# The first two MLP groups run half by half, each half in accumulators of its own; and a new order of x's loads and VectorE's reads

## The chip, the cores and the metric

The kernel runs on one core of a Trainium2 chip. The metric is device time in microseconds (us) of one execution; lower is better. Besides the runs that give the time there is one profiled execution, from which the profile and the trace come. Engines are called by the profile's names: PE (TensorE, matrix products), ACT (ScalarE), DVE (VectorE), POOL (GpSimd) and SP (SyncE, which here only issues DMAs).

## The reference, cut to what matters

A token is a row of 512 numbers; there are 2048. The function normalises x, takes a two-dimensional Fourier transform (real part) by products with the given matrices, puts the same normalised x through an MLP, and joins the two:

```python
xn = _layernorm(x)                                   # x: 2048 x 512
a, b = xn @ dft_hid_re.T, xn @ dft_hid_im.T          # hidden DFT
s = dft_seq_re @ a - dft_seq_im @ b                  # sequence DFT, real part
y = _layernorm(xn)
h = _gelu(y @ w1 + b1)                               # 1792 units
g = _silu(h @ w2 + b2)
return x + s * g
```

## The kernel before, in words

Every fp32 factor is split in two parts, a rounded high one (made by ACT) and the rest as a low one (made by DVE, which needs the high one first); a product is then three matmuls, high by high, high by low and low by high (`split_into`, L63 to L65). The larger products are done in seven block products instead of eight (Strassen's scheme in Winograd's form), so sums and differences of the blocks are made on DVE first.

Tokens come in four blocks of 512, in the order `TB = (0, 2, 1, 3)`. The stages that the change touches, in order:

1. **Hidden DFT of blocks 0 and 2 (of `TB`), L369 to L561.** `x_load` loads x by tiles of 128 tokens, `xt_load` loads transposed blocks. The first four tiles are transposed on PE; the mean and variance of the others come from DVE (`stats`, L110, L111) or, for tokens 12 to 15, from ACT (`act_stats`, L310, L311). A row of means (`m_pack`, `m_turn`: a transpose on PE, a copy on ACT, a write to DRAM from ACT's queue and a load back to all partitions on SP's queue, named `rsm`, `rpm`, `rtm`, `rdm`, `rowm`) is subtracted from the transposed block (L269). `second_factors` (L140) turns the variances into factors, which PE transposes (`rpR`, L166).
2. **Hidden DFT of the other two blocks, L577 to L595**, by seven products of rows (`q_product`, L514), each over four column blocks c. `q_after` reads an accumulator to SBUF (ACT for products 1, 5, 6, 4, DVE L502 for 2, 3, 7). The steps that DVE and ACT do between the products are listed in the calls: `post` (reads), `y_scale`, `y_sum`, `y_split` (the MLP's right factors: "11", "12", "21", "22", and the sums "t1" to "t4", each for the two halves tau = 0 and 1 of the token blocks), `a_split` (weights of the DFT), `w1_sums`, `w1_split`, `w1_load` (the MLP's weights of one group).
3. **MLP, first layer, L599 to L980**: seven groups j of units. A group takes seven products p in the order 1, 5, 6, 2, 3, 7, and 4 later, behind the next group's first two; each is for both halves tau (`TAUS`), twelve matmuls. Products 1, 6, 7, 4 add up in accumulator `hy`, 5 and 3 in `hz`, 2 in `hx`. Behind each `h_product` (L626) stands `h_after`: ACT copies out after products 1, 5 and 6 (L639), DVE adds after 2, 3 and 7 (L669, L675, L679), and ACT applies gelu (L631). Group 0 alone runs by halves, `ONE` (tau 1) and then `ZERO` (tau 0), in the same accumulators, and `y_late` puts the right factors of tau 0 that are not yet made between its products. POOL's queue stores the results, SP's loads and stores the rest.
4. The MLP's second layer, the sequence DFT and the gate follow (L960 to L1141).

The program is run in the order in which it is written (`manual_schedule`): each engine and queue works off its own instructions in that order, and waits where an operand, a buffer or an accumulator is not ready. `yp` has four tiles of two banks for the MLP's accumulators; `wr` holds one group's raw weights; `op` holds 39 tiles that are handed out again when their last user is done.

```python
h_seq = [(0, p, s) for s in (ONE, ZERO) for p in (1, 5, 6, 2, 3, 7)]
for j in range(1, NJ):
    h_seq += [(j, 1, TAUS), (j, 5, TAUS), (j - 1, 4, TAUS), (j, 6, TAUS), (j, 2, TAUS), (j, 3, TAUS), (j, 7, TAUS)]
```

Of the kernel before, what the change touches and what calls it, by code (L numbers as in the profile page):

```python
# [22 lines left out]
def fnet_mixer_kernel(ctx: ExitStack, tc: tile.TileContext, x, xT, ct, wt, w1, w2, b1, b2, out):  # L23
    nc = tc.nc
# [354 lines left out]
    for q in range(NC):  # L379
        x_load(NC + q)  # L380
    for q in (12, 13, 8, 9):
        x_load(q)
    xt_load(1)
    for q in (14, 15, 10, 11):
        x_load(q)
# [12 lines left out]
    m_turn()  # L398
    for q in range(12, 15):
        act_stats(q)  # L400
# [125 lines left out]
    for i in range(3, HB):  # L526
        if i == 3:
            xt_prepare(1)
            act_stats(15)
            for q in (10, 11):  # L530
                stats(mv1, xs[q], q)
            neg_means(2)
            neg_means(0)
        if i == 4:
            second_factors()
        if i == 5:
            a_sums()
# [27 lines left out]

    def w1_make(j):
        w1_sums(j)
        w1_split(j)
        w1_load(j + 1)
# [46 lines left out]

    def h_product(j, p, taus=TAUS):
        key = {1: "y", 2: "x", 5: "z", 3: "z", 6: "y", 7: "y", 4: "y"}[p]
        if (j, key) not in hx:
            hx[j, key] = acc_two(f"h{key}{j}")  # L620
        acc, (wh, wl) = hx[j, key], w1_op[j]
        for tau in range(2)[taus]:
            rh, rl = y_op[RIGHT[p], tau]
            terms = [(w, r, k) for k in range(2) for w, r in ((wh, rh), (wh, rl), (wl, rh))]
            for i, (w, r, k) in enumerate(terms):
                nc.tensor.matmul(acc[:, tau, :], w[:, W1_AT[p], k * P:(k + 1) * P], r[:, k, :],  # L626
                                 start=p in (1, 5, 2) and i == 0, stop=p in (2, 3, 4) and i == len(terms) - 1,
                                 skip_group_check=True)
# [6 lines left out]

    def h_copy(j, key, src, s):
        if (j, key) not in ht:
            ht[j, key] = guest(f"h{key}{j}")
        nc.scalar.activation(ht[j, key][:, s, :], hx[j, src][:, s, :], AF.Copy)  # L639

    def h_sub(j, dst, a, b):
        if (j, dst) not in ht:
            ht[j, dst] = guest(f"h{dst}{j}")
        nc.vector.tensor_sub(ht[j, dst], ht[j, a], ht[j, b])


    def h_after(j, p, s=TAUS):
        whole = s.start == 0
        if p == 1:
            h_copy(j, "c1", "y", s)  # L650
            if j:
                h_sub(j - 1, "t2", "c5", "t1")
                h_store(6, j - 1, ht[j - 1, "t2"])
                h_sub(j - 1, "u2", "c5", "u2")
                h_store(7, j - 1, ht[j - 1, "u2"])
        elif p == 5:
            h_copy(j, "c5", "z", s)
        elif p == 4:
            ht[j, "h21"] = guest(f"h21{j}")
            h_gelu(ht[j, "h21"], hx[j, "y"], j + NJ)  # L660
            h_store(2, j, ht[j, "h21"])
        elif p == 6:
            h_copy(j, "u2", "y", s)
            if j:
                h_last(j - 1)
        elif p == 2:
            ht[j, "h11"] = ht[j, "c1"]
            h11 = ht[j, "h11"][:, s, :]
            nc.vector.tensor_add(h11, h11, hx[j, "x"][:, s, :])  # L669
            h_gelu(h11, h11, j)  # L670
            if j < NJ - 1 and whole:
                h_store(1, j, ht[j, "h11"])
        elif p == 3:
            u2 = ht[j, "u2"][:, s, :]
            nc.vector.tensor_add(u2, u2, hx[j, "z"][:, s, :])  # L675
            h_gelu(u2, u2, j)
        elif p == 7:
            c5 = ht[j, "c5"][:, s, :]
            nc.vector.tensor_add(c5, c5, hx[j, "y"][:, s, :])  # L679
            h_gelu(c5, c5, j + NJ)  # L680
# [278 lines left out]

    for j, p, s in h_seq:  # L960
        if j == 0 and p != 4 and (p, s) in y_late:
            y_late[p, s]()
        h_product(j, p, s)
        if j == NJ - 1:
            last_chunk(p)
        h_after(j, p, s)
        if j == NJ - 1:
# [11 lines left out]
        if 0 < j < NJ - 1 and p in (1, 2, 3):  # L979
            extras[j - 1][{1: 0, 2: 1, 3: 2}[p]]()  # L980

    for u, (p, j) in enumerate(m_units):
# [3 lines left out]
        if u == 1:  # L986

            n = NJ - 1
            h_product(n, 4)
            early.close()  # L990
# [9 lines left out]
        if u == 3:  # L1000
            h_after(n, 4)
        if u == 4:
# [172 lines left out]
```

## Time and profile before

| | us |
|---|---|
| median of 3 runs | 690.09 (689.62 to 690.44) |
| the profiled execution's own time | 690.85 |
| its span, first to last instruction | 688.8 |
| PE busy | 670.0 (97%) |
| DVE busy | 543.7 (79%) |
| ACT busy | 353.4 (51%) |

A row of PE's waits names the waiting line, what it waited for, the total in us, how often and the longest. A row of a timeline has the start and the length in us, engine, line, operation, result and sources, how many were merged, and in brackets the idle time ahead of it with what ended it. A row of the chain of waits has start, length and what held. A window's row has, after its length, the busy us and instructions of PE, PE's weight loads, DVE, ACT and POOL, then the granted clock of PE (1.00 is full), the share of the DMA engines that was busy, and GB/s.

### The profile page before, as it was taken

The page shows a single profiled execution, that of the slowest core. Times are in us where ns is not written, and L with a number is a line of the kernel's source. Part 1 is how long each engine was busy: PE and PEld are TensorE (multiplying, and loading weights), DVE is VectorE, ACT ScalarE, POOL GpSimd, SP SyncE. Part 2 cuts the span into 40 slices and gives each one's busy share as a digit, 9 for nine tenths or more (in the row PEclk, how much of TensorE's full clock was granted, in tenths as well). Part 3 has the DMA queues.
Part 4 walks back from the last instruction along what each step waited for, and adds up shares of the span by engine and source line. Part 5 has one row for each costly group of instructions (what it writes and reads, how often), then busy time and mean ns, then how long its engine had stood idle before and what let it go on. Part 6 is the DMA issues. An engine that isn't in the chain of part 4 may idle for free.

```text
span 688.8 us, 8144 instructions
## 1 busy us (share of the span) xinstructions
PE 670.0 (97%) x2908; PEld 545.7 (79%) x2908; DVE 543.7 (79%) x589; ACT 353.4 (51%) x387; POOL 49.6 (7%) x82
## 2 busy tenths in 40 slices
PE   8999976999999999999999999999999999999996
PEld 5778855888888888888888888888888888888885
DVE  6888894678866696477997999738977479898995
ACT  4735554544444676365454754528444363656540
POOL 1001000121211110000000100000000000120100
PEclk9999997999999999999999999999999999999998
DMA  8868352488898998679879999424554647996983
GB/s 297 295 220 213 124 180 94 184 304 298 304 347 311 370 416 339 241 245 331 298 289 399 394 335 321 137 91 153 199 160 109 154 128 237 305 247 232 327 254 122
DMA packets 70328, 172.26 MB, mean 250 GB/s; under 512 B 6640, under 2 KB 21008, under 8 KB 70288
## 3 DMA queue, kind: packets, MB, share of 16 engines
q1 hardware_dynamic: 58192, 132.40, 55.1%
q0 software_dynamic: 11744, 38.81, 17.8%
q10 hardware_dynamic: 352, 0.54, 0.2%
q8 instruction: 22, 0.36, 0.2%
q14 instruction: 18, 0.15, 0.1%
HBM read 121.38 MB, written 50.35 MB: 249 GB/s over the span
## 4 chain that ended last, share of the span: by engine, by line
PE 88%; DVE 5%; DMA 3%; ACT 2%; issue 1%; SPq 0%; DVEq 0%; ACTq 0%
PE pz L801 19%; PE px L801 17%; PE ma L801 11%; PE hy L626 11%; PE mb L801 8%; PE hz L626 5%; PE pw L801 5%; PE pd L330 3%; PE hx L626 3%; PE px L1119 2%; PE pw L1119 2%; DMA rw<-wt 1%; PE qx L514 1%; PE qy L514 1%; DMA rowm<-rdm 1%
## 5 line engine op out<-in xcount | busy, mean ns | idle before, releaser
L907 DVE TENSOR_TENSOR c<-c,c 128x1024 f32<-128x1024 f32 x32 | 39.0, 1220 | 3.6 <-DMA c<-ct 3.6
L65 DVE TENSOR_TENSOR w1l<-w1r,w1h 128x1792 fp32r<-128x1792 f32 x7 | 14.2, 2026 | 24.9 <-ACT w1h L64 20.0
L65 DVE TENSOR_TENSOR R_b1l<-c,R_b1h 128x1024 fp32r<-128x1024 f32 x16 | 19.5, 1221 | 14.7 <-ACT R_b1h L64 11.4
L801 PE MATMUL pw<-R_s1h,L 128*128 128x512 f32 x96 | 29.7, 389 | 0.0
L64 ACT ACTIVATE R_s3h<-c 128x1024 fp32r<-128x1024 f32 x16 | 17.0, 1062 | 23.7 <-DVE c L907 8.0
L631 ACT ACTIVATE hc<-hc,b_t 128x1024 f32<-128x1024 f32 (+1 forms) x16 | 16.7, 1045 | 22.0 <-DVE hc L669 19.7
L64 ACT ACTIVATE R_b2h<-c 128x1024 fp32r<-128x1024 f32 x16 | 16.9, 1056 | 18.8 <-DVE c L912 14.3
L65 DVE TENSOR_TENSOR R_s2l<-c,R_s2h 128x1024 fp32r<-128x1024 f32 x16 | 19.6, 1222 | 8.6 <-PE pz L801 8.6
L64 ACT ACTIVATE R_s2h<-c 128x1024 fp32r<-128x1024 f32 x16 | 17.0, 1060 | 17.0 <-PE px L801 9.5
L64 ACT ACTIVATE R_b1h<-c 128x1024 fp32r<-128x1024 f32 x16 | 16.6, 1052 | 14.7 <-DMA c<-ct 8.7
L65 DVE TENSOR_TENSOR R_s3l<-c,R_s3h 128x1024 fp32r<-128x1024 f32 x16 | 19.5, 1221 | 4.0 <-PE pz L801 4.0
L64 ACT ACTIVATE R_s1h<-c 128x1024 fp32r<-128x1024 f32 x16 | 16.4, 1052 | 11.7 <-DVE c L918 11.7
L915 POOL DMA_DIRECT2D c<-ct x8 | 7.0, 875 | 202.3 <-issue 148.2
L64 ACT ACTIVATE R_a1h<-c 128x1024 fp32r<-128x1024 f32 x16 | 16.9, 1054 | 8.9 <-PE pz L801 7.2
L801 PEld LDWEIGHTS pw<-R_s1h,L 128*128 128x128 f32 x96 | 18.0, 188 | 3.8
L65 DVE TENSOR_TENSOR R_b2l<-c,R_b2h 128x1024 fp32r<-128x1024 f32 x16 | 19.4, 1219 | 1.5 <-PE px L801 1.5
L65 DVE TENSOR_TENSOR R_a1l<-c,R_a1h 128x1024 fp32r<-128x1024 f32 x16 | 19.5, 1220 | 1.3 <-PE px L801 1.1
L65 DVE TENSOR_TENSOR R_s4l<-c,R_s4h 128x1024 fp32r<-128x1024 f32 x16 | 19.5, 1220 | 0.7 <-PE px L801 0.7
L626 PE MATMUL hy<-yt_1h,w1h 128*128 128x512 f32 x42 | 16.9, 404 | 3.1 <-ACT hc L639 3.1
L912 DVE TENSOR_TENSOR c<-c,c 128x1024 f32<-128x1024 f32 x16 | 19.6, 1224 | 0.4
L64 ACT ACTIVATE R_s4h<-c 128x1024 fp32r<-128x1024 f32 x16 | 16.8, 1050 | 5.0 <-PE pz L801 3.3
L64 ACT ACTIVATE w2h<-w 128x1024 fp32r<-128x1024 f32 (+1 forms) x14 | 13.2, 944 | 11.6 <-DVE w L737 3.9
(949 smaller groups left out, 2228.2 us busy)
## 6 DMA issues: line engine op xcount, KB each, us to landing
c<-ct SPq DMA_DIRECT2D x68, 512.0 KB, 5.5
m<-h_d SPq DMA_DIRECT2D x48, 512.0 KB, 6.5
h_d<-ht POOLq DMA_DIRECT2D x21, 512.0 KB, 7.3
s_d<-sa SPq DMA_DIRECT2D x32, 256.0 KB, 4.0
la<-s_d SPq DMA_DIRECT2D x32, 256.0 KB, 6.3
h_d<-hc POOLq DMA_DIRECT2D x13, 512.0 KB, 4.1
x<-x SPq DMA_DIRECT2D x16, 256.0 KB, 5.6
sa<-a_d SPq DMA_DIRECT2D x8, 512.0 KB, 4.2
```

Source lines behind the costliest of these rows:

```text
L64: nc.scalar.activation(hi, src, AF.Copy)
L65: nc.vector.tensor_sub(lo, src, hi.bitcast(F32))
L330: nc.tensor.matmul(acc, xt[i, k][px], weights[m * NK + k][pw], start=n == 0, stop=n == len(terms) - 1)
L514: nc.tensor.matmul(qx[key, c], a, w, start=p in (1, 5, 2) and n == 0, stop=p in (2, 3, 4) and n == len(terms) - 1, skip_group_check=True)
L626: nc.tensor.matmul(acc[:, tau, :], w[:, W1_AT[p], k * P:(k + 1) * P], r[:, k, :], start=p in (1, 5, 2) and i == 0, stop=p in (2, 3, 4) and ...
L631: nc.scalar.activation(dst, src, AF.Gelu_apprx_tanh, bias=b1_t[:, row:row + 1])
L801: nc.tensor.matmul(acc[k][:, tau, :], a, c[:, tau, :], start=first and i == 0, stop=last and i == len(terms) - 1, skip_group_check=True)
L907: nc.vector.tensor_sub(t, t, raw)
L912: nc.vector.tensor_add(raw, raw, t)
L915: nc.gpsimd.dma_start(out=t, in_=ct[1, 1, n], accum_op=ALU.add)
L1119: nc.tensor.matmul(acc[KEY[name]][k][:, tau, :], a[k], c[:, tau, :], start=False, stop=u == us[-1] and i == 2, skip_group_check=True)
```

## The change

Loads: x's tiles 14, 15, 10 and 11 are loaded after the row of means is asked for, and the transposed block 1 ahead of tiles 12, 13, 8, 9; ACT's statistics of token tile 14 move behind the third transposed tile. In the q products, sums that DVE makes alone move ahead of splits, DVE's reads of product 7 follow each other more closely, and the weights of group 0 are made earlier; those of group 1 are split ahead of the MLP's first product. In the MLP, groups 0 and 1 both run for tau 1 and then both for tau 0; each such part opens accumulators of its own (`hx` is keyed by the part) and uses one bank of each. The right factors of tau 0 are spread over the two parts of tau 1. From group 2 on the order is as before.

```diff
     for q in range(NC):
         x_load(NC + q)
+    xt_load(1)
     for q in (12, 13, 8, 9):
-        x_load(q)
-    xt_load(1)
-    for q in (14, 15, 10, 11):
         x_load(q)
...
     dft_mm(1, 1)
     m_turn()
-    for q in range(12, 15):
+    for q in (14, 15, 10, 11):
+        x_load(q)
+    for q in (12, 13):
         act_stats(q)
     first_factors()
...
             xt_prepare(1)
-            act_stats(15)
+            for q in (14, 15):
+                act_stats(q)
...
-    q_product(5, [then(y_split, "22", 1)], [then(a_split, 3)], [then(y_sum, "t3", 1)], [then(y_split, "t3", 1)])
-    q_product(6, [then(a_split, 7)], [then(y_sum, "t4", 1)], [then(y_split, "t4", 1)])
+    q_product(5, [then(y_split, "22", 1)], [then(y_sum, "t3", 1), then(a_split, 3)], [then(y_split, "t3", 1)])
+    q_product(6, [then(y_sum, "t4", 1), then(a_split, 7)], [then(y_split, "t4", 1)])
...
     q_product(3, [post(3, 0), then(y_scale, 0, 0)], [post(3, 1), then(y_scale, 0, 1)], [post(3, 2)],
-              [post(3, 3), then(y_split, "11", 0)])
-    q_product(7, [then(y_sum, "t1", 0), post(7, 0)], [post(7, 1)], [then(w1_sums, 0), post(7, 2)],
-              [post(7, 3), then(w1_split, 0), then(w1_load, 1)])
-    q_product(4, [then(y_split, "t1", 0)], [then(y_scale, 1, 1), then(y_sum, "t2", 0)], [then(y_scale, 1, 0)],
-              [then(y_split, "t2", 0)])
+              [post(3, 3), then(w1_sums, 0)])
+    q_product(7, [post(7, 0)], [post(7, 1), then(w1_split, 0), then(w1_load, 1)], [post(7, 2)], [post(7, 3)])
+    q_product(4, [then(y_split, "11", 0)], [then(y_sum, "t1", 0), then(y_scale, 1, 1)], [then(y_split, "t1", 0)],
+              [then(w1_sums, 1)])
...
-    def h_product(j, p, taus=TAUS):
-        key = {1: "y", 2: "x", 5: "z", 3: "z", 6: "y", 7: "y", 4: "y"}[p]
-        if (j, key) not in hx:
-            hx[j, key] = acc_two(f"h{key}{j}")
-        acc, (wh, wl) = hx[j, key], w1_op[j]
-        for tau in range(2)[taus]:
+    def h_acc(j, p, s):
+        return hx[j, {1: "y", 2: "x", 5: "z", 3: "z", 6: "y", 7: "y", 4: "y"}[p], s.start, s.stop]
+
+    def h_product(j, p, s):
+        if p in (1, 2, 5):
+            key = {1: "y", 2: "x", 5: "z"}[p]
+            hx[j, key, s.start, s.stop] = acc_two(f"h{key}{j}")
+        acc, (wh, wl) = h_acc(j, p, s), w1_op[j]
+        for tau in range(2)[s]:
...
-    h_seq = [(0, p, s) for s in (ONE, ZERO) for p in (1, 5, 6, 2, 3, 7)]
-    for j in range(1, NJ):
-        h_seq += [(j, 1, TAUS), (j, 5, TAUS), (j - 1, 4, TAUS), (j, 6, TAUS), (j, 2, TAUS), (j, 3, TAUS), (j, 7, TAUS)]
-    y_late = {(1, ONE): lambda: y_split("21", 0),
-              (5, ONE): lambda: y_split("22", 0),
-              (6, ONE): lambda: y_sum("t3", 0),
-              (2, ONE): lambda: y_split("t3", 0),
-              (3, ONE): lambda: w1_make(1),
-              (3, ZERO): lambda: (y_sum("t4", 0), y_split("t4", 0))}
+    h_parts = [(0, ONE), (1, ONE), (0, ZERO), (1, ZERO)] + [(j, TAUS) for j in range(2, NJ)]
+    h_seq, last = [], None
+    for j, s in h_parts:
+        done = last[0] if last and last[1].start == 0 else None
+        h_seq += [(j, p, s, done) for p in (1, 5)] + ([(last[0], 4, last[1], None)] if last else [])
+        h_seq += [(j, p, s, done) for p in (6, 2, 3, 7)]
+        last = j, s
+    y_late = {(0, 1): lambda: (w1_split(1), w1_load(2)),
+              (0, 5): lambda: y_sum("t2", 0),
+              (0, 6): lambda: y_scale(1, 0),
+              (0, 2): lambda: y_split("t2", 0),
+              (0, 7): lambda: y_split("21", 0),
+              (1, 1): lambda: y_split("22", 0),
+              (1, 5): lambda: y_sum("t3", 0),
+              (1, 6): lambda: y_split("t3", 0),
+              (1, 2): lambda: y_sum("t4", 0),
+              (1, 3): lambda: y_split("t4", 0)}
...
-    for j, p, s in h_seq:
-        if j == 0 and p != 4 and (p, s) in y_late:
-            y_late[p, s]()
+    for j, p, s, done in h_seq:
+        if s == ONE and (j, p) in y_late:
+            y_late[j, p]()
         h_product(j, p, s)
...
-        if p == 4 and j + 2 < NJ:
+        if p == 4 and s.start == 0 and j + 2 < NJ:
             w1_sums(j + 2)
             w1_split(j + 2)
```

More of the change, by code (lines that the diff above doesn't have):

```diff
@@ L564, in fnet_mixer_kernel @@
         a_op[p] = [weights[m * NK + 2 * k2 + k] for k in range(2)]
[L566 to L569, printed above, removed]
     def post(p, *cs):
@@ L634, in h_store, with h_place, h_copy, h_after @@
         nc.gpsimd.dma_start(out=h_d[p, j], in_=t)
-    def h_copy(j, key, src, s):
+    def h_place(j, key):
         if (j, key) not in ht:
             ht[j, key] = guest(f"h{key}{j}")
-        nc.scalar.activation(ht[j, key][:, s, :], hx[j, src][:, s, :], AF.Copy)
+        return ht[j, key]
+    def h_copy(j, key, p, s):
+        nc.scalar.activation(h_place(j, key)[:, s, :], h_acc(j, p, s)[:, s, :], AF.Copy)
     def h_sub(j, dst, a, b):
[L642 to L647, printed above, removed]
+        nc.vector.tensor_sub(h_place(j, dst), ht[j, a], ht[j, b])
+    def h_after(j, p, s, done):
+        acc = h_acc(j, p, s)[:, s, :]
         whole = s.start == 0
         if p == 1:
[L650 to L655, printed above, removed]
+            h_copy(j, "c1", p, s)
+            if done is not None:
+                h_sub(done, "t2", "c5", "t1")
+                h_store(6, done, ht[done, "t2"])
+                h_sub(done, "u2", "c5", "u2")
+                h_store(7, done, ht[done, "u2"])
         elif p == 5:
-            h_copy(j, "c5", "z", s)
+            h_copy(j, "c5", p, s)
         elif p == 4:
-            ht[j, "h21"] = guest(f"h21{j}")
-            h_gelu(ht[j, "h21"], hx[j, "y"], j + NJ)
-            h_store(2, j, ht[j, "h21"])
+            h_gelu(h_place(j, "h21")[:, s, :], acc, j + NJ)
+            if whole:
+                h_store(2, j, ht[j, "h21"])
         elif p == 6:
-            h_copy(j, "u2", "y", s)
-            if j:
-                h_last(j - 1)
+            h_copy(j, "u2", p, s)
+            if done is not None:
+                h_last(done)
         elif p == 2:
@@ L668, in h_after @@
             h11 = ht[j, "h11"][:, s, :]
-            nc.vector.tensor_add(h11, h11, hx[j, "x"][:, s, :])
+            nc.vector.tensor_add(h11, h11, acc)
             h_gelu(h11, h11, j)
@@ L674, in h_after @@
             u2 = ht[j, "u2"][:, s, :]
-            nc.vector.tensor_add(u2, u2, hx[j, "z"][:, s, :])
+            nc.vector.tensor_add(u2, u2, acc)
             h_gelu(u2, u2, j)
@@ L678, in h_after @@
             c5 = ht[j, "c5"][:, s, :]
-            nc.vector.tensor_add(c5, c5, hx[j, "y"][:, s, :])
+            nc.vector.tensor_add(c5, c5, acc)
             h_gelu(c5, c5, j + NJ)
@@ L965, in fnet_mixer_kernel @@
             last_chunk(p)
-        h_after(j, p, s)
+        h_after(j, p, s, done)
         if j == NJ - 1:
@@ L978, in fnet_mixer_kernel @@
                 w1_load(j + 3)
-        if 0 < j < NJ - 1 and p in (1, 2, 3):
+        if 0 < j < NJ - 1 and s.start == 0 and p in (1, 2, 3):
             extras[j - 1][{1: 0, 2: 1, 3: 2}[p]]()
@@ L988, in fnet_mixer_kernel @@
             n = NJ - 1
-            h_product(n, 4)
+            h_product(n, 4, TAUS)
             early.close()
@@ L1000, in fnet_mixer_kernel @@
         if u == 3:
-            h_after(n, 4)
+            h_after(n, 4, TAUS, None)
         if u == 4:
```

## The prediction

> **What bounds the kernel now.** I read the page first (busy shares), then TensorE's waits, then stretches of the span by window, then the timelines of TensorE (PE), ScalarE (ACT) and VectorE (DVE) between 13 and 150 us, where the change lies.
>
> ```profile
> span 688.8 us, 8144 instructions
> PE 670.0 (97%) x2908; PEld 545.7 (79%) x2908; DVE 543.7 (79%) x589; ACT 353.4 (51%) x387; POOL 49.6 (7%) x82
> ...
> PE hy L626 <- DVE hc L679: 5.3, 1, 5.3
> PE hy L626 <- ACT hc L639: 3.1, 1, 3.1
> ...
> PE pd L330 <- ACT xt L64: 1.1, 1, 1.1
> ...
> PE qy L514 <- DVE q L502: 0.6, 1, 0.6
> ...
> PE rpR L166 <- DVE rr L124: 0.2, 1, 0.2
> ...
> 150.00:300.00 150.00, 150.00 (x651) 122.04 (x650) 105.55 (x106) 78.79 (x75) 19.14 (x37) 1.00 0.87 325
> ...
> 102.00:104.00 2.00, 2.00 (x6) 1.59 (x5) 1.85 (x2) 0.72 (x3) 0.00 (x0) 0.50 0.74 284
> ...
> 116.00:118.00 2.00, 2.00 (x7) 1.52 (x6) 0.00 (x0) 0.60 (x1) 0.00 (x0) 0.50 1.04 380
> ```
>
> PE is the bound: past the MLP's first group it never idles (150 of 150 us). So time can be won only where PE waits, and all waits that the edits touch stand above: 5.3 and 3.1 in the first MLP group, 0.6 at the last product of the row stage (q), 1.1 and 0.2 in the first DFT stage. Behind the two long ones the granted clock is 0.50, which halves PE. What these cost together, the same stretch shows:
>
> ```profile
> 77.35 0.39 PE L514 MATMUL qz<-A3h,y_1h 128*128 128x512 f32 x1
> ...
> 95.02 0.50 PE L626 MATMUL hy<-y_1h,w1h 128*128 128x512 f32 x1 [0.19 <-ACT q L497]
> ...
> 101.22 0.50 PE L626 MATMUL hy<-yt_1h,w1h 128*128 128x512 f32 x1 [3.14 <-ACT hc L639]
> ...
> 113.96 0.80 PE L626 MATMUL hy<-y_0h,w1h 128*128 128x512 f32 x1 [5.34 <-DVE hc L679]
> ...
> 124.58 0.40 PE L626 MATMUL hy<-y_0h,w1h 128*128 128x512 f32 x1
> ...
> 55.75 5.44 PE qy L514 x24
> ...
> 123.35 4.20 PE hy L626 x18
> ```
>
> From q product 3 (77.35) to the second group (124.58) pass 47.2 us. The work in it is three q products of 5.44 and twelve half products of MLP group 0, each 6 matmuls of 4.20/18 = 0.233, so 1.40: 16.3 + 16.8 = 33.1. **Lost: 14.1 us.** The rest of the kernel is full.
>
> **The change, part by part.**
>
> (a) *x's loads and statistics.* Four of x's loads (14, 15, 10, 11; 1 MB) go behind the row of means on SP's queue, and token 14's ScalarE statistics go behind the third transposed block.
>
> ```profile
> 24.21 0.18 DVE L124 SCALAR_TENSOR_TENSOR rr<-tv,y 128x16 f32<-128x16 f32 x1
> ...
> 24.30 0.62 ACT L310 ACTIVATE squares<-x 128x512 f32<-128x512 f32 x1
> ...
> 25.77 0.67 ACT L356 ACTIVATE e<-pd,rr 128x512 f32<-128x512 f32 x1
> ...
> 26.91 0.59 ACT L64 ACTIVATE xt<-pt 128x512 fp32r<-128x512 f32 x1
> ...
> 27.55 5.73 PE L330 MATMUL pd<-W,xt 128*128 128x512 f32 x24 [1.11 <-ACT xt L64]
> ...
> 29.16 2.36 DVE L269 TENSOR_TENSOR xT<-xT,rowm 128x1024 f32<-128x1024 f32 x2 [0.93 <-DMA rowm<-rdm]
> ...
> 20.81 3.84 DMA rdm<-rtm
> 24.66 4.47 DMA rowm<-rdm
> ...
> 36.52 0.31 ACTq L170 DMA_DIRECT2D rdn<-rtn  x1
> ...
> 37.81 0.32 SPq L174 DMA_DIRECT2D rown<-rdn  x1
> ...
> 20.00:22.00 2.00, 2.00 (x11) 1.57 (x10) 1.83 (x9) 0.90 (x3) 0.00 (x0) 1.00 1.06 389
> ```
>
> ACT spends 25.77 - 24.30 = 1.47 on token 14 ahead of the block that PE waits for at 27.55; moved away, that block comes 1.3 earlier (the factors it queues behind are ready at about 24.4) and the 1.1 wait goes. But PE would only stand at its transpose of the factors (the 0.2 wait) unless DVE's chain, which hangs on the row of means, also comes earlier. That row's write took 3.84 while the DMA engines were full (1.06); the like write of the second row took 37.81 - 36.52 = 1.3. With 1 MB less ahead (2.7 us at 389 GB/s) I expect 1.3 to 2.8, so 1.0 to 2.5 earlier. The bounds for (a) are 0.2 (row not earlier) and 1.3; I take **1.1**, since the row needs only 0.9. The moved loads cost nothing as long as they land before DVE wants tokens 10 and 11, near 32: issued from about 23 on, cover about 3 us. xT's loads for blocks 2 and 3 are queued behind them, 1 MB (2.7 us) later, and are read only behind the second factors and w's sums. The statistics of 14 now precede ACT's copies of that stage by 1.5 us; PE has other banks meanwhile.
>
> (b) *Reorderings in q products 5, 6, 3, 7, 4.* A sum moves ahead of a split that waits for ACT, so DVE fills its waits and gains up to 3 us by product 3; PE is not waiting there. In product 7 the reads of its accumulators now come ahead of DVE's other work, so product 4 finds them read: the **0.6 wait goes** (by the steps below DVE is done with each block 1.1 to 2.9 us ahead of need). It is inside the 14.1.
>
> (c) *The MLP's new order.* Rows that price it:
>
> ```profile
> 92.90 2.03 DVE L65 TENSOR_TENSOR w1l<-w1r,w1h 128x1792 fp32r<-128x1792 f32 x1 [0.50 <-ACT w1h L64]
> 94.84 1.22 DVE L65 TENSOR_TENSOR yt_0l<-xT,yt_0h 128x1024 fp32r<-128x1024 f32 x1
> 95.98 1.22 DVE L447 TENSOR_TENSOR xT<-xT,rowR 128x1024 f32<-128x1024 f32 x1
> ...
> 107.37 0.42 DVE L429 TENSOR_TENSOR w1r<-w1r 128x256 f32<-128x256 f32 x1
> ...
> 108.49 0.42 DVE L432 TENSOR_TENSOR w1r<-w1r 128x256 f32<-128x256 f32 x1
> ...
> 113.22 0.68 DVE L679 TENSOR_TENSOR hc<-hc,hy 128x512 f32<-128x512 f32 x1
> ...
> 91.16 1.70 ACT L64 ACTIVATE w1h<-w1r 128x1792 fp32r<-128x1792 f32 x1 [7.28 <-DVE w1r L432]
> ...
> 93.34 1.05 ACT L64 ACTIVATE yt_0h<-xT 128x1024 fp32r<-128x1024 f32 x1
> ...
> 100.59 0.58 ACT L639 ACTIVATE hc<-hy 128x512 f32<-128x512 f32 x1
> ...
> 107.49 0.73 ACT L631 ACTIVATE hc<-hc,b_t 128x512 f32<-128x512 f32 x1 [0.59 <-DVE hc L669]
> ...
> w1r<-w SPq DMA_DIRECT2D x3, 512.0 KB, 3.6
> ```
>
> The 5.3 was the second half's first product waiting for DVE's last read of the same accumulator, itself behind the weight work of group 1. Now a half has accumulators of its own, and between the halves stand group 1's products: the 5.3 goes. I step the queues in order, with 1.15 per wide DVE step (95.98 - 94.84), 1.5 for w1's four sums, 1.95 for its low part, 0.6 for a half add, and ACT's durations above.
>
> q product 4 runs from 87.1 to 92.6. Its first copy leaves ACT at 89.3; then ACT makes "11" (to 90.3), DVE its low part, t1's sum and "22" to 93.8, t1's low part to 95.0, w1's sums for group 1 to 96.5; ACT rounds those weights to 98.2, and only then copies group 0's first accumulator, to 98.8. PE has finished products 1 and 5 at 95.8, after a wait of about 0.5 for the row stage's last bank: **product 6 waits 3.0** (a new wait in place of the 3.1). w1's load is issued at 88.1, when its buffer is read, lands near 92 by the 3.6 row, and is read at 95.0: cover 3.
>
> Next, DVE: w1's low part to 100.2, t2's sum, "21", t2's split to 103.7, adds to 104.9, low part of "21" (ACT has it behind two gelus) 106.8 to 107.9, add of product 7 to 108.6. PE reaches product 4 of the half at 107.2: **waits 1.4**. ACT then does gelu, "22" and only then group 1's first copy, to 110.8: **0.8**. "22", t3's sum and split, t4's sum, an add and t4's split keep DVE until 120.3, the add of group 1's product 7 ends at 121.0, PE wants it at 119.3: **1.8**. From there the new halves wait for nothing. Group 2's weights are ready at 137.5 for a product at 137.8, slack 0.3; its product 6 waits 0.3. Accumulators: each half group opens three of four slots, and if they are handed out in the order in which they came free, each was read in time. Group 1 in halves means some eight more ACT instructions and three more adds, of half the width (0.58 to 0.73 each): they lie in the queues that I stepped. Sum of (c): 0.5 + 3.0 + 1.4 + 0.8 + 1.8 + 0.3 = **7.8 lost in place of 14.1**.
>
> (d) *The clock.* Unknown for a 3.0 gap. Nearest row: the wait of 3.14 at 101.22, behind which the clock was 0.50. A stretch at half speed of 3.4 us costs 1.7, of which the 1.4 wait later absorbs 1.1: 0.6. Bounds 0 and 2.3 (cold behind the 1.8 wait too, where nothing absorbs it). I take **0.6**.
>
> The Trainium skill, "TensorE: Matmul & The Clock Gate", section on HAM oscillation, says that there should be no PE-idle gaps over about 3.4 us. By it the 3.0 gap would leave the clock alone and the sum be 0.6 better, 682.7. The trace disagrees in part: a 3.14 gap was already followed by half clock.
>
> **Sum.** 14.1 - 7.8 + 1.1 - 0.6 = 6.8 us. The profiled execution took 690.85 (span 688.8), so 684.0; the runs' median is 0.8 below it, so **683.3**.
>
> **Rivals.**
> 1. The row of means comes no earlier: PE is pinned at the factors' transpose, (a) gives 0.2: 684.2. For it: three small transfers in a row set that chain; against: the DMA engines were full at 20 to 22.
> 2. The splits bite harder: half clock twice (2.3) or group 2's weights late beyond their 0.3 slack (each us late is a us on PE, since w1's buffers hold two groups): gain 4 to 5, 685.6. For it: three waits of 1 to 3 us within 26 us.
> 3. Slower: group 1's weights come late. They now stand ahead of the first copy on ACT, so past 3 us of cover each us of w1's landing is a us on PE, and it decides from a delay of 3 + 6.8 = 10 us on. The bound is SP's own wait for w1's buffer before:
>
> ```profile
> SPq L425 <- DVE w1l L65: 20.4, 2, 11.8
> ```
>
> 11.8 later costs 8.8 on PE, with two more stretches of half clock (3.4): 690.1 - 6.8 + 12.2 = 695.5. Against it: the buffer's last reader now ends at 88, and the row stores queued ahead have been computed by 82.
> 4. The halves come apart less than the change says: a group of accumulators is still two banks wide with one in use, so there are four slots for two half groups that want three each. Handed out otherwise than in order of release, group 1 opens at 104.4 in one that DVE reads until 104.9 (0.5), and the second half's product 5 at 117.9 in one read until 120.3 (2.4, of which the 1.8 after it is saved): gain 5.7, 684.4. Against it: past the first group the old order showed no such wait.
>
> **How the numbers follow.** Forecast 0.60 (gain 6 to 7.5), rival 1 0.10, rival 2 0.14, rival 3 0.04, rival 4 0.05, and 0.07 for a clock that stays and waits shorter than stepped (681). The range 681.2 to 686.5 takes in the bounds of (a) and (d) and leaves out rival 3, half of the 0.07, and the tail of rival 2, some 0.15. About 0.2% (1.4 us) is what can be told from no change: faster 0.93, same 0.03, slower 0.04.
>
> **What would show it.** PE's list of waits: no DVE L679 before the second half, ACT L639 of about 3.0 at product 6, two DVE L679 waits of 1.4 and 1.8 before product 4 of each group, ACT L639 of 0.8; none at q product 4, none for xt L64; the row of means landing near 27. Wrong if a wait for w1 or for x appears, or if PE idles past group 2.

## The result, and the profile after

| | before | after |
|---|---|---|
| median of the runs | 690.27 (689.62 to 691.43, 4 runs) | 685.38 (684.43 to 686.5, 4 runs) |
| the profiled execution | 690.85 | 684.43 |
| its span | 688.8 | 682.4 |

The ratio is 0.993 (0.991 to 0.995): 4.9 us faster. The prediction said 683.3 within 681.2 to 686.5; the time lies inside, 2.1 above the number. The gain of 4.9 us in the medians is less than the 6 to 7.5 of the forecast case; the 6.4 of the two profiled executions is in it. The four runs of the changed kernel are spread over 2.1 us, and later sets of it, beside the experiments, gave medians of 685.34, 683.75 and 685.23, at 0.992, 0.991 and 0.993 of before.

The page's head and PE's list of waits, after:

```profile
span 682.4 us, 8159 instructions
...
PE 668.3 (98%) x2908; PEld 543.4 (80%) x2908; DVE 544.2 (80%) x592; ACT 354.0 (52%) x395; POOL 49.7 (7%) x82
```

```profile
PE hy L624 <- ACT hc L640: 3.9, 2, 3.4
PE hy L624 <- DVE hc L679: 2.0, 2, 1.5
```

The 5.3 on DVE's read, the 1.1 on xt, the 0.6 on q and the 0.2 on rr are gone. What is left in the MLP is two waits on ACT's copies (3.4 and 0.5) and two on DVE's adds (1.5 and 0.5). PE's timeline says where, and shows the marks by which the two kernels are compared:

```profile
14.33 2.01 PE L330 MATMUL pd<-W,xt 128*128 128x512 f32 x8
...
22.58 9.49 PE L330 MATMUL pd<-W,xt 128*128 128x512 f32 x40
...
76.05 0.39 PE L514 MATMUL qz<-A3h,y_1h 128*128 128x512 f32 x1
...
92.36 0.40 PE L624 MATMUL hy<-y_1h,w1h 128*128 128x512 f32 x1
...
98.73 0.50 PE L624 MATMUL hy<-yt_1h,w1h 128*128 128x512 f32 x1 [3.41 <-ACT hc L640]
...
108.55 0.39 PE L624 MATMUL hz<-yt_1h,w1l 128*128 128x512 f32 x1
...
109.09 0.50 PE L624 MATMUL hy<-yt_1h,w1h 128*128 128x512 f32 x1
...
111.27 0.50 PE L624 MATMUL hy<-yt_1h,w1h 128*128 128x512 f32 x1 [0.53 <-ACT hc L640]
...
121.44 0.50 PE L624 MATMUL hy<-yt_1h,w1h 128*128 128x512 f32 x1 [1.51 <-DVE hc L679]
...
148.64 0.39 PE L624 MATMUL hx<-y_0h,w1h 128*128 128x512 f32 x1
...
163.31 0.50 PE L624 MATMUL hy<-yt_0h,w1h 128*128 128x512 f32 x1 [0.51 <-DVE hc L679]
...
676.76 0.39 PE L1127 MATMUL px<-R_b1h,L 128*128 128x512 f32 x1
```

The 1.1 us gap in the run of 40 products from 22.58 is closed. At 92.36 the MLP starts right behind the last q product; then come, in the order of the program, product 6 of group 0, its product 4 (109.09), product 6 of group 1, product 4 of group 1, and, new and not foreseen, product 4 of group 2 at 163.31. The same marks in the timeline of before:

```profile
14.24 2.03 PE L330 MATMUL pd<-W,xt 128*128 128x512 f32 x8
...
155.38 0.40 PE L626 MATMUL hx<-y_0h,w1h 128*128 128x512 f32 x1
...
682.73 0.39 PE L1119 MATMUL px<-R_b1h,L 128*128 128x512 f32 x1
```

With 77.35 for q product 3 before, the gain can be booked by stretches, since at each mark the same work has been done (hx at 155.38 and 148.64 is group 2's product 2):

| stretch | predicted | measured |
|---|---|---|
| up to q product 3 | 1.1 | 77.35 - 76.05 = 1.30 |
| from there to group 2's product 2 | 14.1 - 7.8 - 0.6 = 5.7 | (155.38 - 148.64) - 1.30 = 5.44 |
| from there to the last product | 0 | (682.73 - 676.76) - 6.74 = -0.77 |
| behind it, to the end of the span | 0 | 6.4 - 5.97 = 0.43 |
| sum | 6.8 | 6.4 |

The -0.77 is what the wait at 163.31 costs. Its row says 0.51, since it counts idle time from the end of the matmul before, which is 0.39 long, while matmuls otherwise start 0.23 apart; and the matmul behind the wait takes 0.1 more.

The windows after (PE's busy time is the second number, the granted clock the third from the end):

```profile
86.00:130.00 44.00, 38.41 (x156) 29.85 (x155) 28.47 (x31) 24.56 (x33) 0.58 (x1) 0.96 0.34 115
...
98.00:100.00 2.00, 1.27 (x5) 1.09 (x6) 1.77 (x1) 1.17 (x3) 0.00 (x0) 0.94 0.00 0
100.00:102.00 2.00, 2.00 (x6) 1.54 (x6) 2.00 (x3) 1.16 (x2) 0.00 (x0) 0.50 0.33 68
102.00:104.00 2.00, 2.00 (x8) 1.58 (x7) 2.00 (x3) 1.76 (x2) 0.00 (x0) 0.70 0.95 298
```

One stretch at half clock, from about 99.8 to 103.2, as charged. And the queue that makes the 3.41, DVE first, then ACT:

```profile
96.04 0.42 DVE L432 TENSOR_TENSOR w1r<-w1r 128x256 f32<-128x256 f32 x1
...
108.35 0.68 DVE L679 TENSOR_TENSOR hc<-hc,hy 128x512 f32<-128x512 f32 x1
...
120.70 0.68 DVE L679 TENSOR_TENSOR hc<-hc,hy 128x512 f32<-128x512 f32 x1
```

```profile
96.50 1.70 ACT L64 ACTIVATE w1h<-w1r 128x1792 fp32r<-128x1792 f32 x1 [2.19 <-DVE w1r L432]
98.10 0.58 ACT L640 ACTIVATE hc<-hy 128x512 f32<-128x512 f32 x1
```

The first accumulator is full at about 93.8 (92.36 and six steps of 0.23), but its copy stands on ACT behind the rounding of group 1's weights, and that waits for the sums that DVE ends at 96.46. The copy ends at 98.68, and PE goes on at 98.73. The adds at 108.35 and 120.70 end 0.06 ahead of the products at 109.09 and 121.44 that wait for them.

### The profile page after: what moved, and what is told of

It is laid out like the page before. It is cut to its first block, busy times and chain, and to the rows that moved or that the text cites. A ratio compares the mean times of both kernels' runs of the same rounds, so it can differ in the third digit from the quotient of the medians.

```text
span 682.4 us, 8159 instructions
## 1 busy us (share of the span) xinstructions
PE 668.3 (98%) x2908; PEld 543.4 (80%) x2908; DVE 544.2 (80%) x592; ACT 354.0 (52%) x395; POOL 49.7 (7%) x82
## 4 chain that ended last, share of the span: by engine, by line
PE 76%; issue 3%; DVE 1%; POOL 1%; DMA 1%; ACT 0%; POOLq 0%
PE pz L809 19%; PE px L809 18%; PE ma L809 11%; PE mb L809 8%; PE hy L624 7%; PE pw L809 5%; PE hz L624 3%; PE hx L624 2%; PE px L1127 2%; PE pw L1127 2%; POOL h_d L632 1%; DMA h_d<-hc 1%; DVE hc L679 0%; DVE hu L675 0%; DVE yt_0l L65 0%
## 5 line engine op out<-in xcount | busy, mean ns | idle before, releaser
L64 ACT ACTIVATE R_s3h<-c 128x1024 fp32r<-128x1024 f32 x16 | 17.0, 1062 | 23.9 <-DVE c L915 14.1
L629 ACT ACTIVATE hu<-hu,b_t 128x1024 f32<-128x1024 f32 (+1 forms) x9 | 8.7, 963 | 21.7 <-DVE hu L675 21.7
```

The costliest lines, as they stand in the source:

```text
L64: nc.scalar.activation(hi, src, AF.Copy)
L629: nc.scalar.activation(dst, src, AF.Gelu_apprx_tanh, bias=b1_t[:, row:row + 1])
```

## The experiments

Theory: the gain is the long waits less the waits that the new order of ACT's and DVE's queues makes, so what is left can be had by order alone. Rivals: the gain is the loads' and statistics' (a), or the separate accumulators alone, or DVE and ACT are too full in that stretch for any order to help.

**The change again, unchanged (e1_after_again).**

> The changed kernel once more, unaltered, for a second profile and a narrower ratio. The first four runs were 684.4 to 686.5 us, and the profiled one was the fastest. Theory: the change gives the stepped 6.4 to 6.8 us whenever only one stretch of half clock falls into the MLP's start, and slower executions have a second one or a longer one: ratio 0.991 to 0.993, and a profile that is slower than 684.4 shows more half clock near 95 to 122 us. Rival: slower executions lose the time elsewhere (a transfer late in the kernel): then PE's list of waits shows an entry that the first profile did not have.

685.34 (683.28 to 685.62), 0.992 (0.991 to 0.993). The same 3.41 us gap, at 98.81, but its windows show two stretches of half clock, to 104.95 in the timeline:

```profile
98.00:100.00 2.00, 1.19 (x3) 1.00 (x4) 1.70 (x1) 1.24 (x3) 0.00 (x0) 0.53 0.00 0
100.00:102.00 2.00, 2.00 (x7) 1.52 (x6) 2.00 (x3) 0.23 (x1) 0.00 (x0) 0.50 0.38 47
102.00:104.00 2.00, 2.00 (x6) 1.62 (x5) 1.25 (x2) 1.98 (x3) 0.00 (x0) 0.50 0.94 296
104.00:106.00 2.00, 2.00 (x8) 1.53 (x7) 1.17 (x2) 1.34 (x2) 0.00 (x0) 0.76 1.04 400
```

The wait at group 1's product 6 comes 1.3 later than in the first profile (112.59 for 111.27), and the span is 1.2 longer. So the term for the clock is not one number: the same gap costs 1.3 us more in one execution than in another. The rival, a loss elsewhere, falls for this pair: PE's list has no entry that the first profile lacks, and its wait at product 4 of group 2 is 0.43 for 0.51.

**Without the new order of loads and statistics (e1_no_a).**

```diff
-    xt_load(1)
     for q in (12, 13, 8, 9):
         x_load(q)
+    xt_load(1)
+    for q in (14, 15, 10, 11):
+        x_load(q)
...
-    for q in (14, 15, 10, 11):
-        x_load(q)
-    for q in (12, 13):
+    for q in range(12, 15):
         act_stats(q)
...
-            for q in (14, 15):
-                act_stats(q)
+            act_stats(15)
```

> The changed kernel with edit (a) undone: x's loads and ACT's statistics in the old order. Theory: (a) is worth what PE's stage shows, 77.35 - 76.05 = 1.3 us at q product 3, and all behind it moves by that: span 1.3 longer than the changed kernel's, PE's waits of 1.1 (xt L64) and 0.2 (rr L124) back. Rival: PE's later waits in the MLP absorb the shift, since DVE sets them: then 0 to 0.5 us.

685.44 (684.97 to 685.86), beside 685.34 of the change in the same rounds: the times do not tell them apart. The timeline does:

```profile
13.88 2.01 PE L330 MATMUL pd<-W,xt 128*128 128x512 f32 x8
...
27.17 5.74 PE L330 MATMUL pd<-W,xt 128*128 128x512 f32 x24 [1.13 <-ACT xt L64]
...
76.54 0.39 PE L514 MATMUL qz<-A3h,y_1h 128*128 128x512 f32 x1
```

The 1.13 wait is back (the 0.2 at the factors, which was expected too, is not). From the first product of the second token tile (L330) to q product 3 pass 62.66 us, where the change needs 76.05 - 14.33 = 61.72 and before 77.35 - 14.24 = 63.11. So between these profiles (a) is worth 0.9 in its stage, near its 1.1. Over all profiles it is less sure: four without (a), or with only its statistics, need 62.66 to 63.11, eight with it 61.56 to 62.19, but two more with it, e2_warm and e2_w1_late, need 62.84 and 62.81, because PE then waits 0.64 and 0.63 for DVE's read (L502) at q product 5. The rival, that later waits absorb the shift, falls: with two stretches of half clock each, the next stretch takes 73.75 here and 73.84 in e1_after_again. The medians do not show (a), since PE reaches the second tile anywhere from 13.1 to 14.6 in the profiles of this study. It came there at 13.1 to 13.4 where it had waited at most 0.2 for ACT's copies of W (L345 <- ACT W L282), and at 13.7 to 14.6 where it had waited 0.4 to 1.3; in the change's first profile and in e2_warm ACT in turn waited for the loads of W.

**Before, with the statistics of tile 14 moved and nothing else (e1_stats_only).**

```diff
-    for q in range(12, 15):
+    for q in range(12, 14):
         act_stats(q)
...
-            act_stats(15)
+            for q in (14, 15):
+                act_stats(q)
```

> The kernel before with one part of (a) alone: ACT's statistics of token 14 move behind the third transposed tile, x's loads stay where they were. Theory: the wait of 1.1 for the transposed tile goes but PE is pinned at the transpose of the factors, which hang on the row of means (still landing near 29): gain 0.2 us, with new PE waits of about 0.5 for the block xt and 0.6 or more for rr. Rival: the row of means does not pin it, and the gain is 1.1 to 1.3.

689.78 (688.43 to 691.73), 0.999 (0.998 to 1.0). The waits of its profile:

```profile
PE rpn L166 <- DVE nm L301: 0.3, 1, 0.3
...
PE rpR L166 <- DVE rr L124: 0.2, 1, 0.2
```

The xt wait is gone, and PE stands at the transposes of DVE's small factors instead. Without the earlier row of means (a) gains 0.7 between the medians, and 0.33 by the marks (76.95 - 14.17 = 62.78 for 63.11), near the 0.2 expected.

**Before, with accumulators of its own for each half of group 0 and nothing else (e1_own_acc).**

```diff
-        if (j, key) not in hx:
-            hx[j, key] = acc_two(f"h{key}{j}")
...
         for tau in range(2)[taus]:
+            if (j, key, h_part(j, tau)) not in hx:
+                hx[j, key, h_part(j, tau)] = acc_two(f"h{key}{j}")
```

Group 0's gelu behind product 4 becomes two, one for each accumulator.

> The kernel before with accumulators of its own for each half of group 0 and nothing else: group 1 still comes behind both halves. Theory: the 5.3 wait came from the sharing, but DVE and ACT are as late as before, so the second half's product 6 then waits about 4 to 5.6 for the copy of its first accumulator, which stands on ACT behind group 1's weights; stepped gain 3.7 without half clock, 1.5 to 2.5 with it. Rival: the accumulators were all there was to it, and the gain is the 5.3 and its 2.2 of half clock, 7 us or more.

687.77 (687.12 to 688.9), 0.997 (0.995 to 0.998): 2.7 us faster. Its timeline of PE:

```profile
99.76 0.50 PE L633 MATMUL hy<-yt_1h,w1h 128*128 128x512 f32 x1 [3.14 <-ACT hc L646]
...
113.75 0.50 PE L633 MATMUL hy<-yt_0h,w1h 128*128 128x512 f32 x1 [3.77 <-ACT hc L646]
```

The 5.34 on DVE's read is gone, and 3.77 on ACT's copy of the second half has come two products later, a little less than the 4 to 5.6 expected. Of the change's gain the accumulators alone bring about half by the medians (2.7 of 5.2 in these rounds), and 2.15 of 5.44 by the marks from q product 3 to group 2's product 2. The rest came with group 1 in between and the new order of the steps together; no run takes these two apart.

**The change, with tau 0's right factors in another order (e2_reorder).** The copies of products 1 and 5 come ahead of the weights on ACT, sums fill DVE while it waits for ACT, and splits stand behind the adds that free accumulators.

```diff
-    y_late = {(0, 1): lambda: (w1_split(1), w1_load(2)),
-              (0, 5): lambda: y_sum("t2", 0),
...
-              (1, 3): lambda: y_split("t4", 0)}
+    y_late = {(0, 1): lambda: (y_sum("t2", 0), y_scale(1, 0)),
+              (0, 6): lambda: (w1_split(1), w1_load(2), y_split("t2", 0)),
+              (1, 1): lambda: y_sum("t3", 0),
+              (1, 5): lambda: y_split("21", 0),
+              (0, 4): lambda: (y_sum("t4", 0), y_split("t3", 0)),
+              (1, 2): lambda: (y_split("22", 0), y_split("t4", 0))}
```

> The changed kernel with the steps of tau 0 put elsewhere between the same MLP products: t2's sum and "21" ahead of product 1; group 1's weight split and t2's split only ahead of product 6; t3's sum and the split of "21" ahead of group 1's products 1 and 5; t4's sum and t3's split ahead of group 0's product 4; the splits of "22" and t4 ahead of group 1's product 2. No step is added or left out. Theory: what is left of the loss is the order on ACT and DVE alone, splits standing ahead of the copies and adds that PE waits for; stepped through the queues with the measured durations, all the MLP's waits (3.4, 0.5, 1.5 and the one of about 0.5 behind them) go and with them the half clock: 7.0 us below the changed kernel, span near 676, runs near 678, and a smaller spread, since no gap is left to meet the clock's windows. Rival: DVE and ACT are the bound of this stretch whatever the order (DVE 28 of 44 us), and PE's waits only move: gain 0 to 2 us.

676.36 (675.43 to 679.91), 0.981 (0.979 to 0.983). The one row of PE's waits in the MLP, the window, then rows of DVE's and ACT's timelines:

```profile
PE hy L624 <- ACT hu L640: 0.2, 1, 0.2
```

```profile
86.00:130.00 44.00, 43.84 (x189) 34.98 (x189) 33.78 (x39) 28.21 (x38) 3.26 (x6) 1.00 0.50 179
```

```profile
101.06 0.68 DVE L669 TENSOR_TENSOR hc<-hc,hx 128x512 f32<-128x512 f32 x1
```

```profile
93.55 0.59 ACT L640 ACTIVATE hc<-hy 128x512 f32<-128x512 f32 x1
...
95.84 1.71 ACT L64 ACTIVATE w1h<-w1r 128x1792 fp32r<-128x1792 f32 x1 [0.47 <-DMA b_d<-q]
```

In the same 44 us of the span PE is busy for 43.84 (189 matmuls, for 156 in the change), with DVE at 33.8 and ACT at 28.2. The copy starts at 93.55, right behind product 1, for 98.10; the adds behind it (101.06) follow each other. The median is 7.4 below the change's 683.75 in those rounds, where 7.0 was expected. That DVE or ACT bounds the stretch falls: in the profile, what the change left in the MLP was order but for 0.2. The smaller spread that was expected did not come: the five runs lie 4.5 us apart.

**The change, with only group 1's weights moved to product 6 (e2_w1_late)**, to see which step makes the 3.4.

```diff
-    y_late = {(0, 1): lambda: (w1_split(1), w1_load(2)),
+    y_late = {
               (0, 5): lambda: y_sum("t2", 0),
-              (0, 6): lambda: y_scale(1, 0),
+              (0, 6): lambda: (w1_split(1), w1_load(2), y_scale(1, 0)),
```

> The changed kernel with one step moved: group 1's weight split goes from ahead of product 1 to ahead of product 6, behind the two copies. Theory: the 3.4 wait and its half clock go, but the add that product 4 waits for hangs on the same DVE chain and comes no earlier, so about 2.8 us of wait appear there: gain 1.2 to 2.0 us in all. Rival: each wait counts by itself, and the gain is 3.4 and the half clock's 1.5 to 3, about 5 us or more.

682.14 (681.92 to 683.55), 0.989 (0.988 to 0.991), where the change took 683.75 in those rounds. Timeline and a window:

```profile
103.16 0.50 PE L624 MATMUL hz<-yt_1h,w1h 128*128 128x512 f32 x1 [0.86 <-DVE hc L669]
...
107.33 0.50 PE L624 MATMUL hy<-yt_1h,w1h 128*128 128x512 f32 x1 [2.50 <-DVE hc L679]
```

```profile
110.00:112.00 2.00, 2.00 (x6) 1.52 (x6) 1.37 (x2) 1.12 (x2) 0.00 (x0) 0.51 0.00 0
```

The 3.4 at product 6 is gone, 0.86 and 2.50 on DVE's adds come later, with a stretch at half clock of their own: of 3.4 us only 1.6 are won between the medians, as expected (1.2 to 2.0). DVE's queue was the next in line.

**The change, with twelve idle products behind group 0's product 5 (e2_warm)**, into an unused bank, to keep PE busy through the gap.

```diff
         h_product(j, p, s)
+        if j == 0 and p == 5 and s == ONE:
+            for _ in range(12):
+                nc.tensor.matmul(hx[0, "z", 1, 2][:, 0, :], idle[:, :P], idle, start=True, stop=True,
+                                 skip_group_check=True)
```

> The changed kernel with 12 more matmuls of the idle operand behind product 5 of group 0's first half, into the unused bank of its accumulator, so that PE is busy for 2.8 of the 3.4 us in which it waits. Nothing waits for them. Theory: the half clock behind the gap goes in all executions; it cost 1.3 us more in the slower profile (two stretches) than in the faster (one), and PE's later wait on DVE absorbs the first 1.4, so the median falls by 0.5 to 1.5 us and the spread over runs narrows. Rival: the spread comes from elsewhere (the loads at the start), and the median moves by less than 0.4.

Five executions took 682.26 to 686.41, median 683.07, ratio 0.991 (0.989 to 0.993); a sixth took 2397.73, which nothing here explains, and is left out. Its timeline:

```profile
96.67 2.54 PE L974 MATMUL hz<-idle 128*128 128x512 bf16 x11
100.00 0.50 PE L624 MATMUL hy<-yt_1h,w1h 128*128 128x512 f32 x1 [0.80 <-ACT hc L640]
...
109.84 0.50 PE L624 MATMUL hy<-yt_1h,w1h 128*128 128x512 f32 x1 [1.17 <-DVE hc L679]
```

No window between 94 and 118 was below a clock of 1.00. The half clock is gone, and 1.17 at product 4 of group 0 has come in its place, as the prediction had it (1.4, of which a cold stretch hides 1.1). But 683.07 beside 683.75 of the change settles nothing, since the runs of the two overlap, and they did not come closer together. The profiled execution, the slowest of the five, stood for 2.05 at group 2's product 4 (165.57). The marks further down say what the idle products are worth.

**The change a third time, beside these (e2_after_third).**

> The changed kernel unaltered, beside the three others on the same chip, as what they are compared with, and for a third profile. Theory: ratio 0.992 as before; if its profile shows one stretch of half clock behind the 3.4 wait its time is near 684, with two near 685.4.

683.75 (683.37 to 684.34), 0.991 (0.990 to 0.993); 3.40 at product 6, one stretch of half clock, 0.93 at group 2's product 4.

**What makes the wait in group 2.** Ahead of that group's adds stand DVE's sums for the sequence DFT, which read a block (`sa`) loaded back on SP's queue. Its rows in the profiles, in the timelines of DVE and PE:

| profile | DVE waits for the load of sa | PE waits at product 4 of group 2 |
|---|---|---|
| e2_w1_late, e2_reorder, e1_no_a | 2.22, 2.28, 2.34 | none |
| e1_after_again | 2.63 | 0.43 |
| after | 2.74 | 0.51 |
| e2_after_third | 3.15 | 0.93 |
| e2_warm | 4.27 | 2.05 |

PE's wait, where it has one, is DVE's less 2.2. In the profile of before DVE came to these sums without a wait. So they were put behind product 7's add in group 2, in the change (e3_sums_late), in it with the idle products (e3_warm_sums), and in the reordered kernel (e3_reorder_sums), with the change beside them (e3_after_fourth).

```diff
-        if 0 < j < NJ - 1 and s.start == 0 and p in (1, 2, 3):
+        if j == 2 and s.start == 0 and p in (1, 7):
+            for step in {1: (0,), 7: (1, 2)}[p]:
+                extras[j - 1][step]()
+        elif 0 < j < NJ - 1 and j != 2 and s.start == 0 and p in (1, 2, 3):
             extras[j - 1][{1: 0, 2: 1, 3: 2}[p]]()
```

> The changed kernel unchanged, in the same rounds as its variants, so that they are compared on one chip: 683.3 to 686.5, 3.40 at product 6 of group 0 with half clock behind it for one or two stretches of 3.4 us, and 0.4 to 1.0 at product 4 of group 2.

> The changed kernel with one step of group 2 moved: the sums of the sequence DFT (sa, four DVE steps of 0.69) stand behind product 7's add, not behind product 2's. Six profiles showed DVE waiting there for the load of sa for 2.28, 2.63, 2.74, 3.15 and 4.27 us, and PE, at product 4 of group 2, for 0, 0.43, 0.51, 0.93 and 2.05: DVE's wait less 2.2. Theory (the load is late, and the adds behind it pass the wait on): DVE's wait shrinks by about 2.3, PE's wait in group 2 is gone, nothing else moves, median 0.5 to 0.9 below the unchanged kernel of these rounds. Rival (the adds are late by themselves, by the sums' own 2.8 us or the groups' order): a wait of about the same size stays at product 4 of group 2 or comes at group 3, and the median is the same within 0.3.

> Both at once: the twelve idle matmuls behind product 5 of group 0's first half, which keep the clock up, and the sums of sa behind product 7 in group 2. If the half clock (1.7 to 3.4 us of cost, of which 1.1 is given back at the next wait) and the load of sa (0.4 to 2.05) are what makes the changed kernel's executions differ and what holds it above the prediction's sum, the median falls to 681.5 to 682.7 and the executions lie within about 1 us, apart from the start-up's 0.8. If not, it stays at 683 to 684 and as spread as before.

> The reordered kernel (splits of tau 0 behind the copies) with the sums of sa behind product 7 in group 2. In its profile DVE waited 2.28 for the load of sa and PE did not wait; two of its five executions took 677.4 and 679.9 against 675.4 to 676.4 of the others. Theory: those were executions in which the load landed later, so that all executions now lie between 675 and 677, median 675.7 to 676.4. Rival: the load was not it, and one execution in five or so still takes over 677.

| | median | runs | ratio to before |
|---|---|---|---|
| e3_after_fourth | 685.23 | 684.5 to 687.27 | 0.993 (0.992 to 0.995) |
| e3_sums_late | 682.8 | 682.38 to 684.03 | 0.990 (0.988 to 0.992) |
| e3_warm_sums | 683.24 | 682.18 to 683.6 | 0.990 (0.988 to 0.992) |
| e3_reorder_sums | 676.0 | 674.92 to 677.54 | 0.980 (0.979 to 0.982) |

The unchanged kernel was slower here than expected: one run of 687.27 for at most 686.5, and 1.43 at group 2's product 4 for 0.4 to 1.0. DVE's row in e3_after_fourth, and PE's:

```profile
159.02 0.69 DVE L704 TENSOR_TENSOR sa<-sa,sa 128x512 f32<-128x512 f32 x1 [3.66 <-DMA sa<-b_d]
```

```profile
164.21 0.50 PE L624 MATMUL hy<-yt_0h,w1h 128*128 128x512 f32 x1 [1.43 <-DVE hc L679]
```

and DVE's in e3_sums_late, where PE does not wait past 121:

```profile
156.77 1.22 DVE L679 TENSOR_TENSOR hc<-hc,hy 128x1024 f32<-128x1024 f32 x1 [0.71 <-PE hy L624]
159.04 0.68 DVE L704 TENSOR_TENSOR sa<-sa,sa 128x512 f32<-128x512 f32 x1
...
174.82 0.69 DVE L704 TENSOR_TENSOR sa<-sa,sa 128x512 f32<-128x512 f32 x1 [2.57 <-DMA sa<-b_d]
```

3.66 less 1.43 is 2.2 once more. With the sums later, DVE does not wait for the load in group 2, but 2.57 in group 3, whose sums were not moved; in e3_warm_sums it is 3.26 and in e3_reorder_sums 2.75. PE has no wait there in any of the three profiles.

The marks of above in all profiles, as lengths in us, show what each experiment is worth without the start-up. The first column runs from the first product of the second token tile to q product 3, the second to group 2's product 2, the third to the last product; "after" is the change's first profile:

| profiles | to q product 3 | to group 2's product 2 | to the last product |
|---|---|---|---|
| before; e1_stats_only | 63.11; 62.78 | 78.03; 78.08 | 527.35; 527.36 |
| e1_own_acc | 62.73 | 75.88 | 527.35 |
| e1_no_a | 62.66 | 73.75 | 527.75 |
| after; e2_after_third; e3_after_fourth | 61.72; 61.56; 62.01 | 72.59; 72.56; 72.58 | 528.12; 528.55; 529.03 |
| e1_after_again | 61.71 | 73.84 | 528.04 |
| e2_warm; e3_warm_sums | 62.84; 62.01 | 72.05; 72.08 | 529.65; 527.33 |
| e2_w1_late | 62.81 | 70.84 | 527.61 |
| e3_sums_late | 62.19 | 72.57 | 527.35 |
| e2_reorder; e3_reorder_sums | 61.97; 61.98 | 64.85; 64.85 | 527.67; 527.35 |

- *The sums.* With them moved, the third stretch is that of before, 527.35. In the change's four profiles it is 0.7 to 1.7 longer. Between the medians the four small sums won 2.4 us, more than the 0.5 to 0.9 expected; between the two profiles it is 2.1 (spans of 683.3 and 681.2), of which 1.7 lies in the third stretch and the rest ahead of q product 3, where the sums have no part.
- *The idle products.* They are worth 0.5 in the second stretch beside one stretch of half clock (72.6), and about 1.7 beside two (73.8), less than the half clock itself, since the wait for DVE at product 4 of group 0 grows (0.31 to 1.17). The medians do not show it (683.24 beside 682.8), and the forecast for both at once, 681.5 to 682.7, was missed by half a us.
- *The order.* It is worth 7.7 in the second stretch, where stepping the queues had given 7.0; 6.8 lie between the medians with the sums moved in both.

In the reordered kernel the expectation that all executions lie under 677 was not met (677.54). Group 2's wait for the load is gone, that in group 3 is new, and what spreads the executions that were not profiled stays open.

## Why the prediction was right, and what was off

The forecast case held in the profiled execution, which gained 6.4. The median of the runs, 685.38, lies in the slow half of the range, next to rival 2's 685.6; it came there in part by a second stretch of half clock, on which rival 2 had counted, and in part by a wait that no case had. So the mechanism of the forecast is borne out term by term, and that the median still fell inside the range owes something to luck. The steps, one by one:

- *14.1 lost, won back by (b) and (c)*: the 5.3 and the 0.6 are gone, as said. q product 4 finds its banks read. In two of the ten profiles with this order, though, PE stands 0.6 for DVE's read at q product 5 instead, which the prediction did not have.
- *(a), 1.1*: 1.30 up to q product 3, 0.9 by the kernel without it (0.5 to 1.5 over the profiles in which PE does not wait at q product 5). The row of means came earlier: DVE reads it at 26.92 without a wait, for 29.16 behind a wait of 0.93. With the statistics alone, PE waited at the factors. Rival 1 falls.

```profile
26.92 2.35 DVE L269 TENSOR_TENSOR xT<-xT,rowm 128x1024 f32<-128x1024 f32 x2
```

- *(c), the new waits*: product 6 waits 3.41 for 3.0 plus the 0.5 for the row stage's last bank. PE did not wait at 92.36, so it was at product 6 earlier by that 0.5 and stood there longer: it goes on at 98.73, by the steps at 98.8. Product 4 of group 0 stands from 108.78 (108.55 and one step of 0.23) to 109.09, 0.31, for 1.4 less the 1.1 that the half clock hides, so 0.3. Then 0.53 for 0.8, 1.51 for 1.8, and in group 2 some 0.5 in two pieces for 0.3. Rivals 3 and 4 fall: PE's list has no wait for w1 itself and none for an accumulator's slot.
- *(d), 0.6*: right in the first profile, 1.3 more in the second (73.84 for 72.59 in the second stretch). Here rival 2 is true in some executions: the clock stays at half for two stretches, though behind one gap, not behind two as that rival had it. By the Trainium skill ("TensorE: Matmul & The Clock Gate", HAM oscillation) there should be no PE-idle gaps over about 3.4 us. The gaps here measured 3.40 and 3.41, on the rule's edge, and were followed by half clock in all four profiles of the change; the 3.14 of before and of e1_own_acc was, and so was the 2.50 of e2_w1_late, with 0.86 shortly ahead of it. The 2.05 of e2_warm was not. If the length of a gap is what decides, the traces speak for a bound between 2.05 and 2.50 us in this kernel.
- *The term left out*: that PE idles nowhere past group 2. It does, at that group's product 4, by 0.43 to 1.43 in the change's four profiles. The prediction named this as a way to be wrong, but its steps ended with group 2's weights. PE comes to group 2's product 2 6.7 us sooner, and DVE to the sums 4.4 sooner: it wants the load at 159.78 before, without a wait, and at 158.13 - 2.74 = 155.39 after. The load does not come sooner. It stands on SP's queue behind the stores of the sums before (L711), and these start at 140.84 before and at 140.65 after. DVE's and SP's rows, before and after, are

```profile
159.78 0.69 DVE L704 TENSOR_TENSOR sa<-sa,sa 128x512 f32<-128x512 f32 x1
...
147.26 0.36 SPq L700 DMA_DIRECT2D sa<-b_d  x1
```

```profile
158.13 0.69 DVE L704 TENSOR_TENSOR sa<-sa,sa 128x512 f32<-128x512 f32 x1 [2.74 <-DMA sa<-b_d]
...
147.58 2.08 SPq L700 DMA_DIRECT2D sa<-b_d  x1
```

so it is late instead. With that wait taken out the changed kernel takes 682.8, 0.5 below the 683.3 predicted. The wait costs 0.7 to 1.7 in the change's four profiles, and the second stretch of half clock 1.3 in the one that has it. Together they are of the size of what lies between 683.3 and the 685.4 measured; how the first set's slower executions split it is not shown, since they were not profiled.

## What to carry to other kernels

Step the queues in program order over the whole stretch that moves, past the last edited line, up to the first loads that now come late: an earlier consumer makes waits of transfers that were on time. On an engine that both frees accumulators and prepares operands, put the instruction that frees ahead of the preparation; here that order alone was worth 6.8 us, more than the change itself. Moving a late load's reader back can make the next load late in turn, so look at the next group too. Where medians are spread by the start-up, book the gain by marks in the timeline at which the same work has been done.

## What the runs showed of the hardware

- Half clock lasted 3.4 us (99.8 to 103.2) or 6.8 us (98.1 to 104.95) behind the same gap of 3.41. In the second case PE worked again from 98.81 on, so it was busy for 2.7 of the first 3.4 us, which did not end it; the fully busy 3.4 us behind did. The half clock began 0.7 us before the end of the gap in that case and 1.0 us behind it in the other. The Trainium skill (the same page, Part 1) calls the window that decides free-running, which agrees with a cost that changes from one execution to the next.
- Eleven recorded idle products of 2.54 us in all, leaving a gap of 0.80, kept the clock at 1.00.
